# Pooled attention into soft-MoE slots: half-width w2 loads, output groups of four rows, and what goes on SyncE's queue

## The chip, the cores and the metric

The kernel runs on one core of one Trainium2 chip. The metric is the device time of one launch in microseconds (us). Every time below is in us unless it is marked ns.

## The reference

There are two stages. Attention works on 8 batches, 8 heads, 576 positions and 64 features, with keys and values averaged over blocks of 8 positions, so each head has 72 of them. Its output, 4608 rows of 512 features, is the input x of a soft mixture of experts with 8 experts, 4 slots each and 1024 hidden features.

```python
k_p = k.reshape(B, H, Sp, pool, D).mean(axis=3)          # Sp = 72, pool = 8; v_p likewise
scores = scale * np.matmul(q, k_p.transpose(0, 1, 3, 2))
attn = softmax(scores)                                   # over the 72 pooled keys
x = np.matmul(attn, v_p)                                 # -> 4608 rows of 512

logits = x @ phi                                         # 4608 x 32 slots
d = softmax(logits, axis=0)                              # over the rows
slot_input = (d.T @ x).reshape(8, 4, 512)
for e in range(8):
    h = np.maximum(slot_input[e] @ w1[e], 0.0)           # w1[e]: 512 x 1024
    slot_out[e] = h @ w2[e]                              # w2[e]: 1024 x 512
c = softmax(logits, axis=1)                              # over the 32 slots
out = c @ slot_out.reshape(32, 512)                      # 4608 x 512, fp32
```

The inputs are fp32: q, k and v of 9.4 MB each, w1 and w2 of 16.8 MB each, phi of 64 KB. The output is 9.4 MB.

## The kernel before

**Loads.** Every large input goes to SBUF by a DMA that GpSimd (POOL) issues and that casts fp32 to bf16 on the way. Their order is written out by hand and starts with k, q and v of the first pair of batches, then the next pairs, then w1 and w2. `load_pair` (L66) loads one tensor of a pair; k of pair 0 comes in two pieces (`cuts`, L98). `load_w1` (L75) loads one expert, 2 MB at the source. `load_w2` (L80) loads one expert of w2 as 8 rows of 512 columns in each partition, and with `pieces=2` it does so in two column halves, one DMA each. Experts 0 to 3 of w2 reuse the buffers of k, q and v (tag `big`), experts 4 and 5 those of the transposed queries (`qT`), experts 6 and 7 those of the attention output (`xs`). Only expert 7 comes in column halves (L385).

One load is different. SyncE (SP) issues an early piece at the very start (L93): one of the four row blocks of expert 7 of w1, 512 KB, as fp32 into `w1_f`. POOL casts it to bf16 (L102) and only then issues the loads of phi (L105) and of v of pair 0.

**Attention.** Four pairs of batches run one after another (L348). For each, TensorE (PE) pools k and v by matmuls (`pool_stage`), transposes q and computes scores; ScalarE (ACT) exponentiates; VectorE (DVE) normalizes. `place_phi` (L223) needs phi on DVE before the values can be prepared. `combine` adds the pair's part of the dispatch sum and writes its softmax weights over the slots, transposed, into `cT`.

**Experts and output.** After the last pair the order on PE, ACT, DVE and SP is that of the code. All experts' first layer (L427) is computed, then transposed into `hT`. `R_ps` (L446) holds the row sums of the combine softmax, `recR` their reciprocals. The second layer (`second`, L463) accumulates over the experts into two PSUM tiles `so_ps`, one for each half of the 512 columns, in the order in which w2 lands, with some matmuls on zeros (`warm`) between them. For expert 7 the half 0 is done first: `second`, then `slots_out` (L469) scales it into `so`, and then three output groups are written in that half; then the same for half 1.

`output` (L472) writes one group: 256 rows of the output, two consecutive ones in each partition. Two matmuls into `f_ps` (four PSUM buffers), one eviction on DVE and one on ACT into `o_sb` (six buffers), and one DMA on SP's queue. Groups 0 to 2 are written in two column halves (runs of 1 KB in HBM, 256 KB each), groups 3 to 17 in full width (runs of 4 KB, 512 KB each).

Of the kernel before, what the change touches and what calls it, by code (L numbers as in the profile page):

```python
# [8 lines left out]
FP = mybir.dt.float32  # L9
BF = mybir.dt.bfloat16  # L10
AF = mybir.ActivationFunctionType
ALU = mybir.AluOpType
# [6 lines left out]
def kernel(  # L19
# [10 lines left out]
    nc = tc.nc  # L30

    B, H, S, D = q.shape
    POOL = 8
    SP = S // POOL
    DM = H * D
    E = moe_w1.shape[0]
    F = moe_w1.shape[2]
    NS = moe_phi.shape[1]
    SPE = NS // E
    scale = 1.0 / float(D) ** 0.5  # L40
# [4 lines left out]
    NT = S // NI  # L45
    NU = NT // 2
    NR = NT // POOL
    DJ = DM // 128
    FJ = F // 128
    XW = D + NS  # L50
    HQ = H // 2
    NO = B * S // 256
    NG = 128 // NS

    consts = ctx.enter_context(tc.tile_pool(name="consts", bufs=1))
    persist = ctx.enter_context(tc.tile_pool(name="persist", bufs=1))
    big = ctx.enter_context(tc.tile_pool(name="big", bufs=4))
    qpool = ctx.enter_context(tc.tile_pool(name="qpool", bufs=2))
    xpool = ctx.enter_context(tc.tile_pool(name="xpool", bufs=2))
    ps_m = ctx.enter_context(tc.tile_pool(name="ps_m", bufs=2, space=PSUM))  # L60
# [2 lines left out]
    pool_order = ctx.enter_context(ExitStack())  # L63
    pool_order.enter_context(tc.manual_schedule(engines={ET.Pool}))

    def load_pair(src, pair, name, cuts=()):  # L66
        t = big.tile([128, NT, D], BF, name=name, tag="big")
        rows = src[2 * pair:2 * pair + 2].rearrange("b h (i t) d -> (b h i) t d", t=NT)
        for t0, t1 in zip((0,) + cuts, cuts + (NT,)):
            nc.gpsimd.dma_start(out=t[:, t0:t1], in_=rows[:, t0:t1])  # L70
        return t

    w1_sb = persist.tile([128, E, DJ, F], BF)
# [3 lines left out]

    w2_sb = [None] * E

    def load_w2(e, pool, tag, pieces=1):  # L80
        w2_sb[e] = pool.tile([128, FJ, DM], BF, name=f"w2_{tag}", tag=tag)
        src = moe_w2[e].rearrange("(p j) d -> p j d", j=FJ)
        for c in range(pieces):
            cols = slice(c * DM // pieces, (c + 1) * DM // pieces)
            nc.gpsimd.dma_start(out=w2_sb[e][:, :, cols], in_=src[:, :, cols])

    k_sb, q_sb, v_sb = [None] * NP, [None] * NP, [None] * NP


    w1_rows = moe_w1[E - 1].rearrange("(p j) f -> p j f", j=DJ)  # L90
    early = ExitStack()
    w1_f = early.enter_context(tc.tile_pool(name="early", bufs=1)).tile([128, F], FP, name="w1_f")
    nc.sync.dma_start(out=w1_f, in_=w1_rows[:, 0])  # L93


    hT = persist.tile([128, E, FJ, NS], BF)
    nc.vector.memset(hT, 0.0)
    k_sb[0] = load_pair(k, 0, "k_sb", cuts=(4 * POOL,))  # L98
    q_sb[0] = load_pair(q, 0, "q_sb")
    ident = consts.tile([128, 128], BF)  # L100
    make_identity(nc, ident)
    nc.gpsimd.tensor_copy(out=w1_sb[:, E - 1, 0], in_=w1_f)  # L102
    early.close()
    phi_f = persist.tile([128, DM // 128, NS], FP)
    nc.gpsimd.dma_start(out=phi_f, in_=moe_phi.rearrange("(p j) e -> p j e", j=DM // 128))  # L105
    v_sb[0] = load_pair(v, 0, "v_sb")


# [3 lines left out]
    def warm(n, ps):  # L112
        for _ in range(n):
            nc.tensor.matmul(out=ps, lhsT=zeros[:, 0:128], rhs=zeros, start=True, stop=True)  # L114
# [16 lines left out]
    ones = consts.tile([128, 2], BF)  # L131
# [10 lines left out]
    for r in range(2):  # L142
        rows = slice(r * D, (r + 1) * D)
        nc.vector.tensor_copy(out=iphi[rows, :, 0:D],
                              in_=ident[rows, rows].rearrange("p d -> p () d").to_broadcast([D, H, D]))


    cT = persist.tile([128, 2, B * S // 2], BF)
# [4 lines left out]
    nc.vector.memset(siT, 0.0)  # L153
    so = persist.tile([128, DM], BF)
    recC = persist.tile([128, 1], FP)
    recR = persist.tile([128, NO, 2], FP)


    for pair in range(1, NP):
        for dst, src, name in ((k_sb, k, "k_sb"), (q_sb, q, "q_sb"), (v_sb, v, "v_sb")):  # L160
            dst[pair] = load_pair(src, pair, name)
        if pair == NP - 2:
            load_w1(0)
    for e in range(1, E - 1):
        load_w1(e)
    nc.gpsimd.dma_start(out=w1_sb[:, E - 1, 1:DJ], in_=w1_rows[:, 1:DJ])
    for e in range(4):
        load_w2(e, big, "big")


    att = ExitStack()
# [7 lines left out]
    qT = [None] * NP  # L179
    xs = [None] * NP  # L180
# [105 lines left out]
    def logits(x, ee, lg, t0, t1):  # L286

        for h in range(H):
            nc.tensor.matmul(out=lg, lhsT=ident, rhs=x[:, t0:t1, h, D:XW], start=(h == 0), stop=(h == H - 1))  # L289
        nc.scalar.activation(out=ee[:, t0:t1],  # L290
                             in_=lg.rearrange("p t s -> p t () s").to_broadcast([128, t1 - t0, NG, NS]), func=AF.Exp)

# [47 lines left out]
    junk = ps_u.tile([128, 512], FP, name="junk", tag="u")  # L340
# [7 lines left out]
    for pair in range(NP):  # L348
        for qd in range(2):
            if qd == 0:  # L350
                prep = chain(prepare_kq(pair + 1), prepare_v(pair + 1)) if pair + 1 < NP else None
                if pair == 0:
                    prep = chain(prepare_v(0), prep)
            ex = [epool.tile([SP, HQ, 2, S // 2], BF, name=f"ex{b}") for b in range(2)]
            if qd == 0:
                xs[pair] = xpool.tile([128, 9, H, XW], BF, name="xs", tag="xs")
            for i in range(9):
                if i < 8:
                    score_unit(pair, i // 4 * H + qd * HQ + i % 4, ex[i // 4][:, i % 4])
                if i < 5:  # L360
                    if last is not None:
                        u_tile(*last[:2], 4 + i, last[2])
                else:
                    u_tile(pair, qd, i - 5, ex)
                step(prep)
                if pair == 0 and i % 2:
                    step(prep)
                if qd == 0 and pair > 0:
                    if i == 4:
                        comb = combine(pair - 1)  # L370
                        step(comb)
                    if i == 7:
                        step(comb)
                if qd == 1 and i in (2, 6):
                    step(comb)
            if qd == 1:
                for _ in prep or ():
                    pass
            last = (pair, qd, ex)
            if pair == NP - 2 and qd == 1:  # L380
                for e in (4, 5):
                    load_w2(e, qpool, "qT")
            if pair == NP - 1 and qd == 0:
                load_w2(E - 2, xpool, "xs")
                load_w2(E - 1, xpool, "xs", pieces=2)  # L385


    pool_order.close()
# [4 lines left out]
    junk = spare[:, 0]  # L393
# [26 lines left out]
    for n in range(E // NG):  # L420
        for half in range(F // 512):
            cols = slice(half * 512, (half + 1) * 512)
            h_ps = ps_m.tile([128, 512], FP, name="h_ps", tag="m")
            for j in range(DJ):
                for g in range(NG):
                    e = n * NG + g
                    nc.tensor.matmul(out=h_ps[g * NS:(g + 1) * NS],  # L427
                                     lhsT=siT[:, j, e * E:(e + 1) * E].rearrange("p e s -> p (e s)"),
                                     rhs=w1_sb[:, e, j, cols], start=(j == 0), stop=(j == DJ - 1),
# [13 lines left out]
    nc.vector.reciprocal(out=recC, in_=recC)  # L443


    R_ps = ps_m.tile([128, NO, 2], FP, name="R_ps", tag="m")  # L446
    for g in range(NO):
        for r in range(2):
            nc.tensor.matmul(out=R_ps[:, g, r:r + 1], lhsT=cT[:, r, g * 128:(g + 1) * 128], rhs=ones[:, 1:2],
                             start=True, stop=True)  # L450
    nc.vector.reciprocal(out=recR, in_=R_ps)
    att.close()

    opool = ctx.enter_context(tc.tile_pool(name="opool", bufs=6))
    ps_o = ctx.enter_context(tc.tile_pool(name="ps_o", bufs=1, space=PSUM))
    ps_f = ctx.enter_context(tc.tile_pool(name="ps_f", bufs=4, space=PSUM))
    CW = DM // 2
# [3 lines left out]
    def second(e, c):  # L463
        for fj in range(FJ):
            g = fj % NG
            nc.tensor.matmul(out=so_ps[c][g * NS:(g + 1) * NS], lhsT=hT[:, e, fj], rhs=w2_sb[e][:, fj, halves[c]],  # L466
                             start=(e == 0 and fj < NG), stop=(e == E - 1 and fj >= NG), skip_group_check=True)
# [4 lines left out]
    def output(g, cols):  # L472

        w = cols.stop - cols.start
        o_sb = opool.tile([128, 2, w], FP, name="o_sb", tag="o")
        f_ps = [ps_f.tile([128, w], FP, name="f_ps", tag="f") for r in range(2)]
        for r in range(2):
            nc.tensor.matmul(out=f_ps[r], lhsT=cT[:, r, g * 128:(g + 1) * 128], rhs=so[:, cols], start=True, stop=True)  # L478
        nc.vector.tensor_scalar(out=o_sb[:, 0], in0=f_ps[0], scalar1=recR[:, g, 0:1], scalar2=None, op0=ALU.mult)  # L479
        nc.scalar.activation(out=o_sb[:, 1], in_=f_ps[1], func=AF.Copy, scale=recR[:, g, 1:2])  # L480
        nc.sync.dma_start(out=out[g * 256:(g + 1) * 256].rearrange("(p r) c -> p r c", r=2)[:, :, cols], in_=o_sb)


    junk = ps_m.tile([128, 512], FP, name="junk", tag="m")
    for e in range(E - 1):
        for c in range(2):
            second(e, c)
        if e >= E - 3:
            warm(8, junk)
    for c in range(2):  # L490
        second(E - 1, c)
        slots_out(c)
        for g in range(3):
            output(g, halves[c])
    for g in range(3, NO):
        output(g, slice(0, DM))


# [28 lines left out]
```

## Time and profile before

| what | value |
|---|---|
| median of 13 runs | 180.11 us (179.34 to 181.89) |
| the profiled execution, its own time | 179.98 us |
| its span, first to last instruction | 178.0 us |
| PE, DVE, ACT, POOL busy | 138.4, 92.5, 79.8, 19.2 us |
| bytes read from HBM, written to it | 61.93 MB, 9.44 MB |
| share of DMA engine time, POOL's queue | 84.8% |
| share of DMA engine time, SP's queue | 14.6% |
| mean granted TensorE clock | 0.858 |

The page cuts the span into 40 slices of 4.45 us and gives for each the busy tenths of every engine, the mean busy tenths of the 16 DMA engines and the GB/s that they landed. A load that casts counts with its bf16 bytes. In lines of the timeline and of the chain of waits the first two numbers are the start and the duration; in brackets stands how long the engine was idle before and who released it. In the windows table each line is a stretch: its length, the busy time and count of instructions of PE, of PE's weight loads, of DVE, ACT and POOL, then PE's granted clock, the share of DMA time and GB/s. A DMA share can exceed 1 where packets overlap on an engine.

### The profile page before, as it was taken

The numbers are of one execution on the slowest core, as the hardware profiler recorded it, in microseconds if no ns is written. First come the engines' busy times: TensorE is split into PE (matmuls) and PEld (weight loads), VectorE is DVE, ScalarE is ACT, GpSimd is POOL, SyncE is SP. The second block draws the span as 40 slices with busy tenths as digits, with TensorE's granted clock in tenths as the row PEclk, the third lists the DMA queues.
The fourth block names the chain that finished last, engine by engine and source line by source line (L and its number), as shares of the span: only waits on it lengthen the run. The fifth ranks groups of instructions, "written<-read, shape, count | busy, mean of one in ns | idle before, by whom it ended". The sixth has DMA issues, their size and how long they took to land.

```text
span 178.0 us, 3540 instructions
## 1 busy us (share of the span) xinstructions
PE 138.4 (78%) x1467; PEld 85.9 (48%) x1467; DVE 92.5 (52%) x250; ACT 79.8 (45%) x144; POOL 19.2 (11%) x38
## 2 busy tenths in 40 slices
PE   4991799999999999999998987999922276774500
PEld 1361648776886587865865354644811133321100
DVE  6400650279678768869687369643700003876510
ACT  3011146988868679677697440111100002675410
POOL 6501011012110611110011111003000000000000
PEclk9999558999999999999998585589995579999555
DMA  5999999999999999999999999999999996899995
GB/s 150 171 221 225 208 223 211 220 211 221 211 222 212 222 211 219 210 219 214 215 217 214 214 214 219 214 219 215 212 215 221 209 192 81 280 396 404 407 404 229
DMA packets 10094, 40.91 MB, mean 230 GB/s; under 512 B 848, under 2 KB 4432, under 8 KB 6880
## 3 DMA queue, kind: packets, MB, share of 16 engines
q0 software_dynamic: 6144, 30.74, 84.8%
q1 hardware_dynamic: 3936, 9.96, 14.6%
q8 instruction: 11, 0.18, 0.4%
q14 instruction: 3, 0.02, 0.0%
HBM read 61.93 MB, written 9.44 MB: 401 GB/s over the span
## 4 chain that ended last, share of the span: by engine, by line
PE 44%; DMA 34%; ACT 9%; DVE 5%; issue 1%; POOL 1%; ACTq 0%; DVEq 0%
DMA w_xs<-in_moe_w_dram 17%; PE pool_ps L191 9%; PE sc L264 8%; DMA out_dram<-o_sb 7%; DMA phi_f<-in_moe_phi_dram 7%; PE u_ps L277 7%; PE G_ps L295 6%; PE q_ps L206 5%; ACT ex L265 5%; PE lg_ps L289 3%; ACT vp L256 2%; PE fold_ps L217 2%; DVE xs L283 2%; DMA w_f<-in_moe_w_dram 2%; ACT o_sb L480 1%
## 5 line engine op out<-in xcount | busy, mean ns | idle before, releaser
L265 ACT ACTIVATE ex<-sc 72x576 bf16<-72x576 f32 x64 | 38.6, 648 | 12.0 <-PE sc L264 11.1
L283 DVE TENSOR_TENSOR xs<-u_ps,rec 128x384 bf16<-128x384 f32 x72 | 39.4, 552 | 1.5
L277 PE MATMUL u_ps<-vp,ex 72*128 72x97 bf16 (+1 forms) x320 | 27.2, 221 | 1.6 <-DVE xs L283 1.5
L480 ACT ACTIVATE o_sb<-f_ps,recR 128x512 f32<-128x512 f32 (+1 forms) x21 | 12.6, 625 | 31.3 <-PE f_ps L478 27.9
L264 PE MATMUL sc<-qT,kp 64*72 64x288 bf16 x128 | 23.3, 313 | 0.8 <-ACT ex L265 0.7
L277 PEld LDWEIGHTS <-ex 72*128 72x128 bf16 (+1 forms) x320 | 18.2, 107 | 10.8 <-DVE xs L283 3.0
L282 DVE RECIPROCAL rec<-u_ps 128x4 f32<-128x4 f32 x72 | 12.5, 176 | 17.9 <-PE u_ps L277 17.4
L206 PE MATMUL q_ps<-ident,q_sb 128*128 128x128 bf16 x144 | 13.2, 242 | 4.9 <-DMA q_sb<-in_q_dram 4.2
L478 PE MATMUL f_ps<-so,cT 128*128 128x512 bf16 (+1 forms) x42 | 11.6, 371 | 6.8 <-ACT o_sb L480 4.9
L479 DVE TENSOR_SCALAR o_sb<-f_ps,recR 128x512 f32<-128x512 f32 (+1 forms) x21 | 13.6, 672 | 5.7 <-PE f_ps L478 3.1
L206 PEld LDWEIGHTS <-q_sb 128*128 128x128 bf16 x144 | 10.1, 109 | 6.6 <-DMA q_sb<-in_q_dram 4.4
L264 PEld LDWEIGHTS <-kp 64*72 64x72 bf16 x128 | 8.7, 108 | 8.3 <-issue 2.7
L295 PE MATMUL G_ps<-xs,ee 128*128 128x512 bf16 x36 | 11.8, 470 | 0.4 <-ACT ee L290 0.4
L470 DVE TENSOR_SCALAR so<-so_ps,recC 128x256 bf16<-128x256 f32 x2 | 1.0, 484 | 20.9 <-PE so_ps L466 20.9
L114 PEld LDWEIGHTS <-zeros 128*128 128x128 bf16 x53 | 5.9, 118 | 10.9 <-issue 5.8
L290 ACT ACTIVATE ee<-lg_ps 128x1152 bf16<-128x1152 f32 (+3 forms) x6 | 4.9, 811 | 13.5 <-PE lg_ps L289 13.5
L212 DVE COPY qT<-q_ps 128x768 bf16<-128x768 bf16 x16 | 8.8, 551 | 3.9 <-PE q_ps L206 3.7
L210 ACT COPY qT<-q_ps 128x768 bf16<-128x768 bf16 x8 | 6.4, 797 | 9.9 <-PE q_ps L206 9.8
L194 ACT CAST kpar<-pool_ps 128x512 bf16<-128x512 f32 (+1 forms) x12 | 5.5, 485 | 11.7 <-PE pool_ps L191 11.6
L478 PEld LDWEIGHTS <-cT 128*128 128x128 bf16 x42 | 4.0, 97 | 13.8 <-issue 11.3
L191 PE MATMUL pool_ps<-pmat,v_sb 128*128 128x128 bf16 x144 | 10.2, 227 | 0.0
L191 PE MATMUL pool_ps<-pmat,k_sb 128*128 128x128 bf16 x144 | 9.9, 219 | 0.3 <-DMA k_sb<-in_k_dram 0.2
(81 smaller groups left out, 155.2 us busy)
## 6 DMA issues: line engine op xcount, KB each, us to landing
out_dram<-o_sb SPq DMA_DIRECT2D x15, 512.0 KB, 5.0
w_sb<-in_moe_w_dram POOLq DMA_DIRECT2D x7, 1024.0 KB, 32.5
q_sb<-in_q_dram POOLq DMA_DIRECT2D x4, 1152.0 KB, 18.1
v_sb<-in_v_dram POOLq DMA_DIRECT2D x4, 1152.0 KB, 17.3
w_big<-in_moe_w_dram POOLq DMA_DIRECT2D x4, 1024.0 KB, 37.2
k_sb<-in_k_dram POOLq DMA_DIRECT2D x3, 1152.0 KB, 20.7
w_qT<-in_moe_w_dram POOLq DMA_DIRECT2D x2, 1024.0 KB, 36.2
out_dram<-o_sb SPq DMA_DIRECT2D x6, 256.0 KB, 2.6
```

The costliest lines, as they stand in the source:

```text
L191: nc.tensor.matmul(out=ps[:, r].rearrange("p n i -> p (n i)"), lhsT=src[:, tt:tt + 2, :].rearrange("p t d -> p (t d)"), rhs=pmat, start=(t ...
L206: nc.tensor.transpose(out=ps[:, t].rearrange("p n i -> p (n i)"), in_=q_sb[pair][:, tt:tt + 2, :].rearrange("p t d -> p (t d)"), identity= ...
L212: nc.vector.tensor_copy(out=dst, in_=ps)
L264: nc.tensor.matmul(out=ps[:, r, 0:S // 2], lhsT=kp[pair][rows, n], rhs=qT[pair][rows, n], start=True, stop=True)
L265: nc.scalar.activation(out=dst.rearrange("p r (i t) -> p r i t", t=NU), in_=ps[:, :, 0:S // 2].rearrange("p r (t i) -> p r i t", i=NI), fu ...
L277: nc.tensor.matmul(out=ps[rows, hh], lhsT=ex[b][:, hh].rearrange("p r t -> p (r t)")[:, c:c + rows.stop - rows.start], rhs=vp[(2 * pair + ...
L282: nc.vector.reciprocal(out=rec, in_=ps[:, :, XW])
L283: nc.vector.tensor_tensor(out=xs[pair][:, t, qd * HQ:(qd + 1) * HQ, :], in0=ps[:, :, 0:XW], in1=rec.rearrange("p h -> p h ()").to_broadcas ...
L295: nc.tensor.matmul(out=ps, lhsT=ee[:, t].rearrange("p g s -> p (g s)"), rhs=x[:, t, :, 0:D], start=(t == 0), stop=(t == 8))
L478: nc.tensor.matmul(out=f_ps[r], lhsT=cT[:, r, g * 128:(g + 1) * 128], rhs=so[:, cols], start=True, stop=True)
L479: nc.vector.tensor_scalar(out=o_sb[:, 0], in0=f_ps[0], scalar1=recR[:, g, 0:1], scalar2=None, op0=ALU.mult)
L480: nc.scalar.activation(out=o_sb[:, 1], in_=f_ps[1], func=AF.Copy, scale=recR[:, g, 1:2])
```

## The change

- The early piece of w1 is gone from SP's queue, with its buffer and POOL's cast; expert 7 of w1 is loaded whole by POOL like the others. phi is loaded by SP at the start instead. k of pair 0 is loaded in one piece, and `hT` is not cleared.
- Of the last two experts of w2, which have 8 rows each in a partition, 11 of the 16 rows are loaded in column halves: five rows of expert 6 in full width, then half 0 of its other three and of expert 7, then half 1 of both. In the second layer the two experts are taken half by half.
- Five groups of 256 rows are written in halves where three were. One group of 256 rows follows in full width. The other 3072 rows make six groups of 512 rows, four consecutive ones in each partition, so that a run in HBM is 8 KB and a DMA 1 MB; their buffers are slices of `w1_sb`.

```diff
-    w1_rows = moe_w1[E - 1].rearrange("(p j) f -> p j f", j=DJ)
-    early = ExitStack()
-    w1_f = early.enter_context(tc.tile_pool(name="early", bufs=1)).tile([128, F], FP, name="w1_f")
-    nc.sync.dma_start(out=w1_f, in_=w1_rows[:, 0])
+    phi_f = persist.tile([128, DM // 128, NS], FP)
+    nc.sync.dma_start(out=phi_f, in_=moe_phi.rearrange("(p j) e -> p j e", j=DM // 128))
...
-    nc.vector.memset(hT, 0.0)
-    k_sb[0] = load_pair(k, 0, "k_sb", cuts=(4 * POOL,))
+    k_sb[0] = load_pair(k, 0, "k_sb")
...
-    nc.gpsimd.tensor_copy(out=w1_sb[:, E - 1, 0], in_=w1_f)
-    nc.gpsimd.dma_start(out=phi_f, in_=moe_phi.rearrange("(p j) e -> p j e", j=DM // 128))
...
+    def load_last_w2(pool, tag):
+        j = FJ - 3
+        src = [moe_w2[e].rearrange("(p j) d -> p j d", j=FJ) for e in range(E)]
+        for e in (E - 2, E - 1):
+            w2_sb[e] = pool.tile([128, FJ, DM], BF, name=f"w2_{tag}", tag=tag)
+        nc.gpsimd.dma_start(out=w2_sb[E - 2][:, 0:j], in_=src[E - 2][:, 0:j])
+        for c in range(2):
+            cols = slice(c * DM // 2, (c + 1) * DM // 2)
+            nc.gpsimd.dma_start(out=w2_sb[E - 2][:, j:FJ, cols], in_=src[E - 2][:, j:FJ, cols])
+            nc.gpsimd.dma_start(out=w2_sb[E - 1][:, :, cols], in_=src[E - 1][:, :, cols])
...
-    for e in range(1, E - 1):
+    for e in range(1, E):
         load_w1(e)
-    nc.gpsimd.dma_start(out=w1_sb[:, E - 1, 1:DJ], in_=w1_rows[:, 1:DJ])
...
-                load_w2(E - 2, xpool, "xs")
-                load_w2(E - 1, xpool, "xs", pieces=2)
+                load_last_w2(xpool, "xs")
...
+    groups = []
+    for n in [2] * NSMALL + [4] * ((NO - NSMALL) // 2):       # NSMALL = 6, NHALF = 5
+        row0 = sum(128 * g[1] for g in groups)
+        step_ = n // 2
+        rows = lambda r, c0=row0 // 2, s=step_: cT[:, r % 2, c0 + r // 2:c0 + 128 * s:s]
+        groups.append((row0, n, rows))
...
+    nc.vector.memset(R_ps, 1.0)
+    for g, (_, n, rows) in enumerate(groups):
+        for r in range(n):
+            nc.tensor.matmul(out=R_ps[:, g, r:r + 1], lhsT=rows(r), rhs=ones[:, 1:2], start=True, stop=True)
...
     def output(g, cols):
         w = cols.stop - cols.start
+        row0, n, rows = groups[g]
+        if n == 4:
+            o_sb = w1_sb[:, g - NSMALL].rearrange("p j f -> p (j f)").bitcast(FP).rearrange("p (r c) -> p r c", r=n)
+        else:
+            o_sb = opool.tile([128, n, w], FP, name=f"o_sb{w}", tag=f"o{w}", bufs=2 if w == DM else 2 * NHALF)
+        for r in range(n):
+            f_ps = ps_f.tile([128, w], FP, name="f_ps", tag="f")
+            nc.tensor.matmul(out=f_ps, lhsT=rows(r), rhs=so[:, cols], start=True, stop=True)
+            if r % 2:
+                nc.scalar.activation(out=o_sb[:, r], in_=f_ps, func=AF.Copy, scale=recR[:, g, r:r + 1])
+            else:
+                nc.vector.tensor_scalar(out=o_sb[:, r], in0=f_ps, scalar1=recR[:, g, r:r + 1], scalar2=None,
+                                        op0=ALU.mult)
+        nc.sync.dma_start(out=out[row0:row0 + 128 * n].rearrange("(p r) c -> p r c", r=n)[:, :, cols], in_=o_sb)
...
-    for e in range(E - 1):
+    for e in range(E - 2):
         for c in range(2):
             second(e, c)
-        if e >= E - 3:
+        if e == E - 3:
             warm(8, junk)
     for c in range(2):
+        second(E - 2, c)
+        if c == 0:
+            warm(6, junk)
         second(E - 1, c)
         slots_out(c)
-        for g in range(3):
+        for g in range(NHALF):
             output(g, halves[c])
-    for g in range(3, NO):
+    for g in range(NHALF, len(groups)):
         output(g, slice(0, DM))
```

## The prediction

> **What bounds the kernel now.** I read the page's slices first. The DMA row stands at 9 from slice 2 to 33 and again from 36 to 39, with a dent between, and the bytes say what kind of time that is: about 215 GB/s landed while inputs come in (cast from fp32 to bf16, so twice that is read), about 405 GB/s while the output goes out. PE is as full in the middle, so I asked next who waits at the end.
>
> ```profile
> PE   4991799999999999999998987999922276774500
> DMA  5999999999999999999999999999999996899995
> GB/s 150 171 221 225 208 223 211 220 211 221 211 222 212 222 211 219 210 219 214 215 217 214 214 214 219 214 219 215 212 215 221 209 192 81 280 396 404 407 404 229
> ```
>
> In the chain of waits the last long link is a weight load, and stores follow it to the end. The PE rows of the timeline show the same: from w2's expert 3 on, each second-layer block starts when its load lands.
>
> ```profile
> 120.96 30.27 DMA w_xs<-in_moe_w_dram
> 151.28 0.43 PE so_ps L466 x8
> ...
> 136.24 1.05 PE L466 MATMUL so_ps<-w_qT,hT 128*32 128x256 bf16 x16 [4.23 <-DMA w_qT<-in_moe_w_dram]
> 141.10 1.04 PE L466 MATMUL so_ps<-w_qT,hT 128*32 128x256 bf16 x16 [3.81 <-DMA w_qT<-in_moe_w_dram]
> 148.65 0.40 PE L466 MATMUL so_ps<-w_xs,hT 128*32 128x256 bf16 x8 [0.18 <-DMA w_xs<-in_moe_w_dram]
> 151.28 0.40 PE L466 MATMUL so_ps<-w_xs,hT 128*32 128x256 bf16 x8 [0.29 <-DMA w_xs<-in_moe_w_dram]
> ```
>
> So the kernel is one stream of loads followed by one stream of stores, and what remains to be won lies at its three edges. The windows table (the last two numbers are DMA share and GB/s) prices them:
>
> ```profile
> 0.00:2.00 2.00, 0.00 (x0) 0.00 (x0) 0.98 (x2) 1.27 (x1) 0.96 (x6) 1.00 0.13 29
> 2.00:3.20 1.20, 0.94 (x3) 0.39 (x4) 1.17 (x11) 0.22 (x2) 1.20 (x3) 1.00 0.88 311
> 148.60:151.90 3.30, 1.78 (x22) 0.90 (x21) 1.99 (x5) 1.31 (x3) 0.00 (x0) 1.00 0.20 26
> 151.90:154.20 2.30, 1.60 (x9) 0.88 (x10) 1.84 (x5) 1.31 (x3) 0.00 (x0) 1.00 0.96 337
> 154.00:155.00 1.00, 0.66 (x3) 0.19 (x2) 1.00 (x2) 0.75 (x3) 0.00 (x0) 1.00 0.81 273
> 170.00:176.00 6.00, 0.00 (x0) 0.00 (x0) 0.00 (x0) 0.00 (x0) 0.00 (x0) 0.50 1.02 406
> ```
>
> **Start**: the early piece on SyncE's queue fills 1.8 to about 3.7 us. **Turn**: from 148.6 to 151.9 the DMA engines stand at 0.20. Half 0 of the last expert has landed (PE starts at 148.65) but its first store moves only at 151.9, 3.26 us later: PE, so, PE, o_sb until SP's issue at 150.66, then 1.25 us of store latency. **Stores**: 154 to 155 holds a gap of about 0.2 us between the half-0 and half-1 stores, and half-width stores (runs of 1 KB) go at 337 to 348 GB/s against 405 for full-width ones (4 KB).
>
> **What the Trainium skill says.** "DMA: Bandwidth & Descriptors", Issuing engines are not separate DMA queues: all queues end on the same 16 engines. The trace agrees: share 0.88 with SP's piece alone, 0.94 at 3.2 to 4.2 with both queues, so the piece pays only while POOL's stream is not there. The same page, Specifications: first byte about 1 us for POOL's path, 0.6 for SP's; here SP took 1.07 us (0.73 to 1.80), and POOL's own delay is hidden behind SP's packets. "Perfetto Trace Analysis", DMA Optimizations: larger pieces fill HBM bandwidth better, naming 2 KB to 4 or 8 KB; the trace agrees from 1 to 4 KB and has no 8 KB store. The first page, Where 436 GB/s comes from, puts a ceiling of 435 GB/s on what 16 engines move; no stretch here is above it once casts are counted at the source.
>
> **The change, part by part.**
>
> 1. *Early piece off SP.* 512 KB of w1 join POOL's stream. A whole w2 expert (2 MB at the source) takes 141.10 - 136.24 = 4.86 us, so a quarter costs +1.22 us. phi (64 KB) leaves that stream for SP's empty start: 4.86/32 = -0.15. POOL's cast of the piece (1.04 us) and its 0.58 us wait go, and the memset of hT (0.91 us on DVE) goes; each lies beside the loads and is worth nothing by itself.
>
> 2. *When POOL's stream starts.* Before, no slice between the two queues is empty, so the trace does not show when POOL's first descriptors were ready. Its issue is at 1.24 us. Earliest: 1.24 + the page's 1 us = 2.24; latest: as now, 3.3 to 3.7. That is a gain of 0 to 1.3 us. I take 0.5, below the middle, because the last engine decides and the share of 0.86 at 4 to 5 us says that some engines get POOL's work late even now.
>
> 3. *Column halves.* Of the last two experts' 16 rows, 8 came in halves; now 11. Eight half-rows took 151.28 - 148.65 = 2.63 us where half an expert at full width takes 2.43, so six more half-rows add 6/8 x 0.20 = +0.15. Sum of 1 to 3: loads end 1.22 - 0.15 - 0.5 + 0.15 = **+0.7 us** (-0.1 to +1.2). The distance between the landings of half 0 and half 1 grows to 11/8 x 2.63 = 3.62, so half 0 lands at +0.7 - 0.99 = **-0.3 us**, and with it the first store (3.26 us after it, the same six steps). POOL's last five DMAs, not three, are issued while over 15 us of loads are still queued (29 to 38 us from issue to landing in the tail), also where each waits for the one eight before it to land.
>
> 4. *PE order at the turn.* Expert 6's half 1 and expert 7's half 1 stand behind ten f_ps matmuls in PE's order. Those wait on four f_ps buffers, so on evictions: 10 evictions on DVE and ACT, 0.47 us each, five in a row from 1.42 us after the landing, the last matmul at about 2.9. Half 1 lands at 3.62: not late. The six warm matmuls (0.21 to 0.43 us each, 1.3 to 2.6) fit into the 2.63 us between expert 6's and expert 7's half.
>
> 5. *Half-width stores, ten in place of six.* SP issues one each 0.65 us (0.60 plus its wait), a 256 KB store at 346 GB/s lasts 0.76, so SP keeps up. The five of half 0 last until 3.26 + 3.8 = 7.06 us after the landing; half 1's first store is ready 3.62 + 3.07 = 6.69 after it (3.07 = 154.35 - 151.28: eviction to 152.59, issue at 153.1, latency 1.25). The 0.2 us gap closes, with 0.4 to spare. Four more half stores: 1.05 MB x (1/346 - 1/405) = +0.44 us.
>
> 6. *Runs of 8 KB.* Twelve full-width groups become six of 1 MB: 6.29 MB, 15.53 us at 405 GB/s. Per engine a 1 KB run costs 1024/(346/16) = 47 ns, a 4 KB run 162: 26.9 bytes per ns and 9 ns fixed. Two of 4 KB cost 324, one of 8 KB 314: -2.8%, **-0.44 us**. Ends: nothing, if rows are cut to 4 KB; -1.07 if the ceiling of 435 were reached; above zero see the last rival. Four evictions stand ahead of each store (DVE 2 x 0.75), 1.5 us against 2.6 us of transfer, and w1_sb as their buffer was read last at 125 us, so no wait on buffers. The first of them is issued about 1.3 us before the stores ahead of it run out.
>
> 7. *Rest.* R_ps's memset comes after recC in DVE's order and pushes the R matmuls and the second layer from 128.1 to about 129.3; the load that PE awaits lands at 131.40. k in one piece lets pooling begin some 1.5 us later (11.3 before; the second piece landed 10.8 us after its issue at about 1.9); q, which PE waits for next, lands at 2.46 + 15.7 = 18.2 in any case, and DVE's 12.2 us wait for phi is gone. POOL's loads are issued over 7 us ahead of their turn, so a late release starves nothing. The cT weights are now read with a step of two, by a PE that is idle half the time from 160 on. All zero.
>
> Sum: turn -0.3, gap -0.2, half stores +0.44, long runs -0.44: **-0.5 us**. Against its own time, 179.98 us (span 178.0 and 1.98 around it), that is 179.5; the median of 13 is 180.11, 0.13 above, so I predict 179.6. A measurement can tell about 0.5% here, 0.9 us: this is no change that it would see.
>
> **Rivals.**
> - *POOL starts at once* (faster). All engines get its stream at 2.2 to 2.5: loads end at +0.0, half 0 lands 1.0 earlier, stores -0.2 more: -1.2, 178.9; with 8 KB runs near the ceiling 178.2. For: POOL issues at 1.24, and SP's packets may be all that holds it. Against: the uneven 4 to 5 us.
> - *The engines drift further apart* (slower). Landings wait for the slowest of 16. At the end the share falls from 1.26 at 147.5 to 0.32 at 149.5, yet half 1 lands at 151.2: a spread of some 3 us. SP's piece gave the engines that POOL reaches late something to do. If the spread grows, both landings slip by it and the stores with them: at 1.5 us, -0.5 + 1.5 = +1.0, 181.1. It decides from 1.4 us. Against: nothing in the change touches the engines' shares of work.
> - *The long runs are no longer runs*: the queue cuts them to 4 KB, and the -0.44 is gone: 180.05, no change. If 8 KB stores fell below 371 GB/s (15.53 to 16.9 us) the result would be slower; nothing here speaks for it.
>
> **How the numbers follow.** Forecast 0.50, its own range 178.9 to 180.3; early start 0.25; drift 0.16; cut runs 0.09. Faster by over 0.5% (under 179.2): 0.25 and 0.09 of the forecast's lower edge, 0.34. Slower (over 181.0): the drift and a little of other errors, 0.18. Within: 0.48. The range 178.4 to 181.2 leaves out the ceiling case and more drift than priced.
>
> **What would show it.** Right: POOL's stream begins before 3.3 us; half 1's PE block starts at about 152.0, half 0's at 148.3; first store at 151.6; no slice under 0.9 from there; 10 half stores at 346 GB/s and the six long ones at 415. Wrong: a distance of over 4 us between the landings (then a gap opens), loads ending over 1.2 us later, or long runs at 405 or less.

## The result, and the profile after

The changed kernel took 178.05 us (median of 11 runs, 178.0 to 179.25) against 180.29 us for the kernel before (48 runs). The ratio is 0.9887, 95% interval 0.9863 to 0.9911. On a second occasion it was 178.16 against 180.48, ratio 0.9924 (0.9900 to 0.9948). The ratios leave out executions that took over 1.5% longer than the fastest of their kernel (21 of 62 of the kernel before on the second occasion), so they are not the quotients of the medians. By them the change is worth 2.0 us on the first occasion and 1.4 on the second. The forecast was 179.6, no measurable change, within 178.4 to 181.2. The kernel became about 1% faster and fell below that range. The profiled execution took 178.02 us for a span of 176.2.

The page's slices show the same shape as before, loads and then stores. The dent between them is no longer visible in the DMA row, which stays at 9, and slice 34 lands 145 GB/s where it landed 81.

```profile
DMA  4999999999999999999999999999999999999995
GB/s 76 205 224 211 226 205 220 211 216 219 215 218 211 223 211 220 210 218 218 218 208 218 221 212 212 218 218 216 212 216 219 201 196 145 317 361 425 417 417 208
```

The DMA row from 140 to 152 us, 0.3 us a digit, shows that the dent is smaller and not gone: from 148.7 to 150.2 us the engines are still busy for three to four tenths only. In the kernel before it was 0.20 for 3.3 us.

```profile
DMA  9899999999999999999999999999843333999999
```

The timeline of PE, DVE and SP at the turn (start, duration, engine, line) gives the landings.

```profile
140.05 1.05 PE L472 MATMUL so_ps<-w_qT,hT 128*32 128x256 bf16 x16 [3.80 <-DMA w_qT<-in_moe_w_dram]
...
146.79 0.40 PE L472 MATMUL so_ps<-w_xs,hT 128*32 128x256 bf16 x8 [0.18 <-DMA w_xs<-in_moe_w_dram]
147.31 0.48 DVE L476 TENSOR_SCALAR so<-so_ps,recC 128x256 bf16<-128x256 f32 x1 [20.13 <-PE so_ps L472]
...
148.82 7.65 SPq L495 DMA_DIRECT2D out_dram<-o_sb  x11
150.02 0.79 PE L472 MATMUL so_ps<-w_xs,hT 128*32 128x256 bf16 x16
150.86 0.48 DVE L476 TENSOR_SCALAR so<-so_ps,recC 128x256 bf16<-128x256 f32 x1 [0.35 <-PE so_ps L472]
```

Expert 5 of w2 lands at 140.05, where it landed at 141.10, although POOL's stream now carries 512 KB more. Half 0 follows at 146.79 in place of 148.65. SP's first store is issued 2.03 us after that, as before (2.01). `so` of half 1 comes 3.55 us after `so` of half 0, where it came 2.57 us after (149.16 and 151.73). So in these two profiles the kernel is ahead by 1.05 us before anything of the turn has begun, and by 1.86 us at half 0.

The windows table of the changed kernel (last two numbers: DMA share, GB/s) shows the start and the stores:

```profile
0.00:2.00 2.00, 0.82 (x2) 0.28 (x3) 1.11 (x11) 1.27 (x1) 0.97 (x6) 1.00 0.03 10
2.00:3.20 1.20, 1.20 (x4) 0.46 (x3) 0.33 (x3) 0.21 (x2) 1.12 (x4) 1.00 1.07 137
150.00:157.00 7.00, 5.40 (x38) 2.30 (x38) 6.17 (x12) 5.35 (x11) 0.00 (x0) 1.00 1.00 339
158.00:170.00 12.00, 3.87 (x14) 1.14 (x12) 5.03 (x8) 4.78 (x8) 0.00 (x0) 0.82 1.02 420
170.00:174.00 4.00, 0.00 (x0) 0.00 (x0) 0.00 (x0) 0.00 (x0) 0.00 (x0) 0.50 0.99 414
```

Half-width stores run without a gap at 339 GB/s (344 from 151 us on, when no load is left), and the 8 KB runs at 414 to 420 GB/s, where the 4 KB runs had 404 to 406.

The gain at the start can be read where PE first waits for q of pair 0, the second load that POOL issues. The trace records a landing of q for each of the 16 DMA engines. In the changed kernel the last of them is at 15.97 us and PE starts on q at 16.02: it waits for the slowest engine. The kernel before:

```profile
18.24 1.46 PE L206 MATMUL q_ps<-ident,q_sb 128*128 128x128 bf16 x12 [4.23 <-DMA q_sb<-in_q_dram]
```

The changed kernel:

```profile
16.02 4.27 PE L206 MATMUL q_ps<-ident,q_sb 128*128 128x128 bf16 x33 [3.29 <-DMA q_sb<-in_q_dram]
```

That is 2.22 us. Less the piece's 1.22 us, which POOL loads later, and with the 0.15 us of phi that it no longer loads, 1.15 is left, and 1.05 is what expert 5 shows.

The 16 landings tell where it comes from. "Middle" is the median of the 16 engines, "last" the slowest.

| profile | q, middle | q, last | expert 5, middle | expert 5, last |
|---|---|---|---|---|
| before | 15.85 | 18.20 | 138.74 | 141.06 |
| before, second profile | 15.48 | 18.14 | 138.17 | 140.99 |
| changed | 14.73 | 15.97 | 138.62 | 140.01 |
| changed, second profile | 14.75 | 15.72 | 138.57 | 140.06 |

At q the middle engine is 1.12 us earlier: POOL's first packets start at 2.62 us in place of 3.30, and the piece's are not among them. By expert 5 that is used up, since the piece has to be loaded after all: the middle engine stands at 138.62 against 138.74. What stays is the lag of the last engine behind the middle one, 2.35 us at q before and 1.24 after. From q to expert 5 the first and the last engine drift apart by a further 0.9 to 2.3 us in every profile, so one landing of expert 5 is not exact: with the start of the changed kernel it lies between 139.85 and 140.73 in eight profiles. q is the surer sign.

### The profile page after: what moved, and what is told of

Same layout as the page of the kernel before. It is cut to its first block, busy times and chain, and to the rows that moved or that the text cites. A ratio compares the mean times of both kernels' runs of the same rounds, so it can differ in the third digit from the quotient of the medians.

```text
span 176.2 us, 3525 instructions
## 1 busy us (share of the span) xinstructions
PE 137.8 (78%) x1469; PEld 86.0 (49%) x1469; DVE 90.6 (51%) x252; ACT 79.9 (45%) x146; POOL 18.5 (10%) x37
## 4 chain that ended last, share of the span: by engine, by line
PE 49%; DMA 25%; ACT 13%; DVE 4%; issue 2%; POOL 0%; ACTq 0%; DVEq 0%; POOLq 0%
DMA w_xs<-in_moe_w_dram 17%; PE pool_ps L191 9%; PE sc L264 8%; DMA q_sb<-in_q_dram 8%; PE u_ps L277 7%; PE G_ps L295 6%; PE q_ps L206 6%; ACT ex L265 5%; PE f_ps L489 3%; PE lg_ps L289 3%; ACT w_sb L491 2%; ACT vp L256 2%; DVE xs L283 2%; PE fold_ps L217 2%; ACT o_sb L491 2%
## 5 line engine op out<-in xcount | busy, mean ns | idle before, releaser
L491 ACT ACTIVATE o_sb<-f_ps,recR 128x256 f32<-128x256 f32 (+1 forms) x11 | 5.2, 492 | 26.8 <-PE f_ps L489 26.8
L489 PE MATMUL f_ps<-so,cT 128*128 128x512 bf16 (+1 forms) x46 | 11.0, 331 | 3.5 <-DVE so L476 1.2
L472 PEld LDWEIGHTS <-hT 128*32 128x32 bf16 x128 | 3.5, 104 | 13.0 <-issue 12.8
L191 PEld LDWEIGHTS <-v_sb 128*128 128x128 bf16 x144 | 9.0, 104 | 0.8 <-issue 0.2
```

The source lines that it names most:

```text
L191: nc.tensor.matmul(out=ps[:, r].rearrange("p n i -> p (n i)"), lhsT=src[:, tt:tt + 2, :].rearrange("p t d -> p (t d)"), rhs=pmat, start=(t ...
L489: nc.tensor.matmul(out=f_ps, lhsT=rows(r), rhs=so[:, cols], start=True, stop=True)
L491: nc.scalar.activation(out=o_sb[:, r], in_=f_ps, func=AF.Copy, scale=recR[:, g, r:r + 1])
```

## The experiments

The question was where the 2 us came from: from the start, the turn or the long runs, and which of the start's four edits it was. Each kernel below is the changed kernel with one thing put back, unless said otherwise.

**Old start.** All four edits of the start undone.

```diff
-    nc.sync.dma_start(out=phi_f, in_=moe_phi.rearrange("(p j) e -> p j e", j=DM // 128))
+    nc.sync.dma_start(out=w1_f, in_=w1_rows[:, 0])
+    nc.vector.memset(hT, 0.0)
-    k_sb[0] = load_pair(k, 0, "k_sb")
+    k_sb[0] = load_pair(k, 0, "k_sb", cuts=(4 * POOL,))
+    nc.gpsimd.tensor_copy(out=w1_sb[:, E - 1, 0], in_=w1_f)
+    nc.gpsimd.dma_start(out=phi_f, in_=moe_phi.rearrange("(p j) e -> p j e", j=DM // 128))
...
```

> The changed kernel with the old start alone: early piece of w1 on SP's queue, phi on POOL's, k of pair 0 in two pieces, hT cleared. Theory A (the gain is mainly at the start: POOL's stream begins earlier and its slowest engine catches up, by more than the early piece was worth): w2's expert 5 lands at about 141.1 us again instead of 140.05, all later steps follow by about 1.05, ratio to the kernel before about 0.9945 (179.3 us). Theory B (the start is worth nothing, the turn and the long runs brought all of it): ratio stays at 0.988 to 0.989.

Measured: 179.24 us, ratio 0.9959 (0.9934 to 0.9985). Its PE rows:

```profile
17.85 1.46 PE L216 MATMUL q_ps<-ident,q_sb 128*128 128x128 bf16 x12 [4.20 <-DMA q_sb<-in_q_dram]
...
141.83 1.04 PE L482 MATMUL so_ps<-w_qT,hT 128*32 128x256 bf16 x16 [3.87 <-DMA w_qT<-in_moe_w_dram]
```

q is late again and so is expert 5. Theory A holds: the start is worth some 1.1 us by the medians (179.24 against 178.05 to 178.16) and 0.6 to 1.3 us by the ratios, about half of the gain or more. But single runs went from 177.83 to 180.72, so some executions with the old start were as fast as the changed kernel.

**Old turn.** Expert 7 alone in halves, three half-width groups, warm matmuls as before.

```diff
-    NHALF = 5
+    NHALF = 3
-        j = FJ - 3
+        j = FJ
...
```

> The changed kernel with the old turn alone: expert 7 of w2 in column halves only, three groups in half width, six rows of warm matmuls back where they were. From the prediction's own terms the first store comes 0.99 us later after the loads, the 0.2 us gap is back and four half stores fewer give 0.44 back: +0.75 us against the changed kernel, ratio to before about 0.993 (178.8 us). A rival, that the turn is hidden by something else and worth nothing: 0.989.

Measured: 179.67 us, ratio 0.9985 (0.9961 to 1.0009), far more than expected. The timeline and the window of that run show that the edit had made a new wait:

```profile
158.41 0.69 ACT L490 ACTIVATE o_sb<-f_ps,recR 128x512 f32<-128x512 f32 x1 [2.43 <-DMA out_dram<-o_sb]
158.43 0.75 DVE L492 TENSOR_SCALAR o_sb<-f_ps,recR 128x512 f32<-128x512 f32 x1 [2.73 <-DMA out_dram<-o_sb]
```

```profile
158.00:160.00 2.00, 0.86 (x3) 0.29 (x3) 1.57 (x3) 1.27 (x2) 0.00 (x0) 0.61 0.53 215
```

With three half-width groups, three groups of 256 rows follow in full width, and `opool` has only two buffers for them. Both evicting engines stand still until a store gives one back, and DMA falls to 0.53. So it was run again with a third buffer.

```diff
-bufs=2 if w == DM else 2 * NHALF
+bufs=3 if w == DM else 2 * NHALF
```

> As the run with the old turn (expert 7 of w2 alone in column halves, three groups in half width), but with three buffers for the three full-width groups of 256 rows in place of two. In that run DVE and ACT stood still for 2.7 and 2.4 us at 158.4, until a store gave its buffer back, and DMA at 0.53 from 158 to 160; about 0.9 us of store time were lost so. Without it: +0.75 us against the changed kernel, by the prediction's terms, ratio to before 0.991 to 0.994. If the ratio stays at 0.9985, the turn is worth twice what the prediction said.

Measured: 178.29 us, ratio 0.9912 (0.9887 to 0.9937). The turn by itself is worth 0.1 to 0.25 us by the medians, where the prediction's terms made 0.75. Against the two ratios of the changed kernel it is +0.45 and -0.2 us, so it is not clear of zero.

**Runs of 4 KB.** Twelve groups of 256 rows in the same buffers.

```diff
-    NSMALL = 6
+    NSMALL = NO
...
```

> The changed kernel with twelve full-width groups of 256 rows (runs of 4 KB, 512 KB a store) in the same buffers in place of the six of 512 rows. If the fixed cost per run is the cause: stores at 405 GB/s in place of 415 to 419, +0.44 to +0.6 us, ratio to before 0.991 to 0.992. If the long runs bring nothing: 0.989.

Measured: 178.2 us, ratio 0.9916 (0.9885 to 0.9947), which does not stand clear of the changed kernel; the span is 176.4. Its windows:

```profile
158.00:170.00 12.00, 3.85 (x14) 1.10 (x12) 5.01 (x8) 4.76 (x8) 0.00 (x0) 0.85 1.02 405
170.00:174.00 4.00, 0.00 (x0) 0.00 (x0) 0.00 (x0) 0.00 (x0) 0.00 (x0) 0.50 1.02 406
```

The rate is the one expected, 405 in place of 414 to 420. But the time is not all there. The DMA rows from 172 to 176 us, 0.1 us a digit, with each packet counted where it starts, show where each kernel's packets run out. The changed kernel:

```profile
DMA  1991997999799799799000000000000000000000
```

With runs of 4 KB:

```profile
DMA  9996999959979999699698995800000000000000
```

By their records the last packets end at 174.2 and at 174.8 us, but the spans at 176.2 and 176.4. Of 0.6 us of store time only 0.2 reach the end. After the last packet the changed kernel goes on for 2.0 us, the other for 1.6. The reason for that difference was not tried, and the length of the stores is not it alone: with the same stores of 1 MB at the end, both runs of the old turn went on for only 1.3 us.

**More halves.** 14 of the last 16 rows in halves, six half-width groups.

```diff
-        j = FJ - 3
+        j = FJ - 6
-    NHALF = 5
+    NHALF = 6
```

> The changed kernel with 14 of the last 16 rows of w2 in column halves and six half-width groups. The landings of the two halves stand 14/8 x 2.63 = 4.6 us apart, half 0 lands 0.85 us earlier and the first store with it, while loads still run on the slower engines. If the stretch with idle engines at the turn is filled so: up to -0.6 us against the changed kernel (ratio to before 0.985 to 0.987). If the stores only take the bandwidth that the last loads need, or more 1 KB runs eat it up: 0.989 or above.

Measured: 177.85 us, ratio 0.9896 (0.9854 to 0.9939), no difference from the changed kernel.

```profile
144.90 1.87 PE L116 MATMUL junk<-zeros 128*128 128x512 bf16 x6
146.71 0.40 PE L472 MATMUL so_ps<-w_xs,hT 128*32 128x256 bf16 x8
...
151.04 0.40 PE L472 MATMUL so_ps<-w_xs,hT 128*32 128x256 bf16 x8 [0.27 <-DMA w_xs<-in_moe_w_dram]
```

Half 0's block starts at 146.71, hardly before the changed kernel's 146.79, and half 1's waits for DMA until 151.04. The blocks did move apart, by 4.33 us (4.6 expected), but mostly because half 1 moved back. Half 0's last landing is recorded at 146.4, 0.3 us before its block, which starts when the warm matmuls end. Eight half-rows took 2.63 us in the kernel before where full rows take 2.43, and the last loads now run beside the first stores, which begin at 150.0. No more was to be won here from halving more than 11 rows.

**The start, edit by edit.** Four kernels put back one of its edits each, and two put back the piece with one partner each.

```diff
 piece_back:    nc.sync.dma_start(out=w1_f, in_=w1_rows[:, 0]) ahead of phi; POOL's cast
 cuts_back:     k_sb[0] = load_pair(k, 0, "k_sb", cuts=(4 * POOL,))
 memset_back:   nc.vector.memset(hT, 0.0)
 phi_on_pool:   nc.gpsimd.dma_start(out=phi_f, ...) behind q, nothing on SP's queue
 piece_cuts, piece_memset: two of these together
```

> The changed kernel with the early piece of w1 alone put back: SP loads it first, phi behind it on SP's queue; k in one piece, no memset of hT. Theory A1 (SP's packets stand ahead of POOL's on each engine and hold POOL's stream until 3.3 us and later, most on the engines that POOL reaches last): first POOL packets at 3.2 to 3.4 in place of 2.6, k's landing spread over the engines by about 3 us in place of 1.6, w2's expert 5 at 141.1 to 141.8 us in place of 140.05, ratio to before 0.994 to 0.996. Theory A2 (the memset of hT or the two pieces of k delayed POOL's stream, and the piece itself only filled empty time): expert 5 at 139.0 to 139.3, ratio 0.983 to 0.985.

> The changed kernel with k of pair 0 in two pieces again, nothing else. A1: the stream starts at 2.6 as in the changed kernel, expert 5 lands within 0.5 us of 140.05, ratio 0.987 to 0.990. A2 with the pieces as the cause: slowest engine 1 to 2 us later, ratio 0.994.

> The changed kernel with the memset of hT on DVE again (0.91 us from about 1 us on, while POOL writes its first descriptors), nothing else. A1: no effect, expert 5 within 0.5 us of 140.05, ratio 0.987 to 0.990. A2 with the memset as the cause: POOL's first packets at 3.2 us or later, expert 5 up to 1 us later, ratio 0.993.

> The changed kernel with nothing on SP's queue at the start and phi on POOL's queue behind q. A1, with any SP packets at the start as the cause: POOL's stream starts earlier still than 2.6 us; otherwise it starts at 2.6 and phi adds 0.15 us: expert 5 at 140.2, ratio 0.988 to 0.991.

> The changed kernel with the early piece on SP's queue and k of pair 0 in two pieces, without the memset. Alone neither delayed the loads (expert 5 at 139.78 and 140.33 us against 140.05), all of the old start together did (141.83). Theory C1 (it takes both: three POOL loads stand behind SP's packets on each engine when they start, and some engines are served late): k whole on the slowest engine at about 12 us in place of 10.2, expert 5 at 141 us or later, ratio to before 0.992 to 0.996. Theory C2 (it takes the memset or phi on POOL's queue): expert 5 at 139.8 to 140.4, ratio 0.983 to 0.988.

> The changed kernel with the early piece on SP's queue and the memset of hT, k in one piece. C1: like the piece alone, expert 5 at 139.8 to 140.3, ratio 0.983 to 0.988. C2 with the memset as the partner: expert 5 at 141 or later, ratio 0.992 to 0.996.

The landings of q and of expert 5 are the starts of PE's blocks, as in the lines above. In the first two rows phi is on POOL's queue too.

| kernel | piece on SP | k in two | memset | q of pair 0 | expert 5 | median us | ratio (95%) |
|---|---|---|---|---|---|---|---|
| before | yes | yes | yes | 18.24 | 141.10 | 180.29 | |
| old start | yes | yes | yes | 17.85 | 141.83 | 179.24 | 0.9959 (0.9934 to 0.9985) |
| piece and two pieces of k | yes | yes | no | 18.25 | 142.08 | 178.31 | 0.9921 (0.9896 to 0.9946) |
| piece and memset | yes | no | yes | 18.14 | 141.98 | 177.81 | 0.9872 (0.9828 to 0.9916) |
| piece | yes | no | no | 16.34 | 139.78 | 177.89 | 0.9832 (0.9790 to 0.9873) |
| k in two pieces | no | yes | no | 15.40 | 140.33 | 177.92 | 0.9850 (0.9816 to 0.9883) |
| memset | no | no | yes | 15.89 | 140.98 | 179.02 | 0.9893 (0.9849 to 0.9937) |
| phi on POOL | no | no | no | 15.93 | 140.11 | 178.23 | 0.9875 (0.9838 to 0.9911) |
| changed | no | no | no | 16.02 | 140.05 | 178.05 | 0.9887 (0.9863 to 0.9911) |

The profiled executions of the two kernels with one partner took 180.11 and 180.16 us, about 2 us above their medians, so their landings are shown but decide nothing. Without any of the piece, q lands by 16.13 in every profile, those of the other experiments included. With the piece alone it lands 0.3 us later than in the changed kernel, and since POOL's later loads are 1.22 us shorter, expert 5 is even early. Half of theory A1 holds for the piece alone: POOL's first packets start later, at 3.57 us in place of 2.62 (3.2 to 3.4 foretold). But the engines finished k 1.25 us apart and not 3, and expert 5 was not late. A2 falls too, for neither the memset nor the two pieces of k delays q. With all the edits of the old start together q is 1.8 to 2.2 us late in each of three profiles (18.24 and 17.85 here, 18.18 below). Which combination it takes, C1 or C2, stays open: by its ratio neither pair stands clear of the changed kernel, and no run has the piece with phi on POOL's queue alone.

**Repeats.** Since single runs of the kernels with the piece scattered, three kernels were run once more.

> The changed kernel again, as the yardstick for the three others. Ratio to before 0.987 to 0.990, all its runs within about 1.3 us of each other (178.0 to 179.25 before); k whole on the slowest engine at about 10.2 us, spread over the engines at most 1.6 us, as in all nine profiles without the early piece.

> The changed kernel with the early piece alone put back, again. The kernels with the piece ran from 176.8 to 180.7 us, those without it within 0.5 to 1.3 us of their median, and of five profiles with the piece four had some engines 2.3 to 2.8 us behind the first when k had landed, this one 1.3. Theory D1 (the piece makes the start uneven in some executions and not in others, so that its 1.22 us are won or lost by chance): times again spread over 2 us or more on both sides of the changed kernel's, median within 0.3% of it. Theory D2 (the piece alone is harmless and worth its bytes, only its combination with the two pieces of k or the memset costs): every run under the changed kernel's, ratio 0.980 to 0.984, spread under 1.4 us.

> The kernel before, a second profile of it. D1: its slowest engine again 2 us or more behind at the landing of k, or not at all, and w2's expert 5 within 139.5 and 142 us accordingly. If the start is the same in every execution: expert 5 at 141.10 again, within 0.2 us. Ratio to itself 0.998 to 1.002.

The changed kernel came out at 178.16, its runs from 177.8 to 178.91, q at 15.77. The kernel before came out at 179.9, its runs from 178.64 to 181.59, ratio to itself 1.0017 (0.9988 to 1.0045); q at 18.18 and expert 5 at 141.03. That is within 0.1 us of its first profile. So both profiles of the kernel before start late; whether all its executions do is not shown, since its times go from 178.1 to 182.75 us. The piece alone:

```profile
16.04 0.84 PE L213 MATMUL q_ps<-ident,q_sb 128*128 128x128 bf16 x12 [3.31 <-DMA q_sb<-in_q_dram]
...
139.51 1.05 PE L479 MATMUL so_ps<-w_qT,hT 128*32 128x256 bf16 x16 [3.94 <-DMA w_qT<-in_moe_w_dram]
```

177.86 us, runs from 177.3 to 179.61, ratio 0.9904 (0.9871 to 0.9937). In both profiles of the piece alone expert 5 is 0.3 to 0.5 us early. Its middle engine is 0.6 to 0.7 us early (137.88 and 137.98 against 138.62), so the piece does pay there. But the kernel's times scatter over 2.3 us where the changed kernel's scatter over 1.1. D1 is nearer than D2: the median is 0.2% under the changed kernel's and single runs lie on both sides of it.

**Half a piece, and piece with more halves.**

```diff
 half_piece:   nc.sync.dma_start(out=w1_f, in_=w1_rows[:, 0:F // 2])
 piece_halves: piece_back with  j = FJ - 6  and  NHALF = 6
```

> The changed kernel with an early piece of half the size (256 KB of w1, phi behind it on SP's queue), k in one piece. In the changed kernel POOL's first packets start at 2.6 us and SP's queue can move data from about 1.75, so this piece fills just the empty stretch. If the piece pays as far as it ends before POOL's stream starts: POOL's first packets at 2.7 to 3.0, k's spread under 1.6 us, expert 5 at about 139.6, 0.4 to 0.6 us under the changed kernel, times within 1.5 us of each other, ratio to before 0.985 to 0.988. If any SP packet at the start delays POOL's stream by as much as it carries: as the changed kernel, 0.988 to 0.992.

> The changed kernel with the whole early piece back (k in one piece, no memset) and with 14 of the last 16 rows of w2 in halves and six half-width groups: the two edits that stood at or under the changed kernel's time. If both add: 0.3 us for the piece, 0.2 for the halves, ratio to before 0.984 to 0.988, single runs from 176.8 to 179.5 as with the piece. If the start's scatter and the stores' lower rate eat them up: 0.988 to 0.992.

Measured: half the piece 178.24 us, ratio 0.9877 (0.9835 to 0.9919), q at 16.36, expert 5 at 139.81. Piece and more halves 177.87 us, ratio 0.9868 (0.9825 to 0.9911), q at 17.05, expert 5 at 140.86. Neither stands clear of the changed kernel, and the two edits do not add. In the second kernel the piece came back alone, and q was still 1 us late, with the engines 2.0 us apart. So the piece by itself can make the start uneven, if less than the whole old start. No version was found that surely beats the changed kernel.

**The new start in the kernel before.** The other direction: the kernel before with the new start alone.

```diff
-    nc.sync.dma_start(out=w1_f, in_=w1_rows[:, 0])
+    nc.sync.dma_start(out=phi_f, in_=moe_phi.rearrange("(p j) e -> p j e", j=DM // 128))
-    nc.vector.memset(hT, 0.0)
-    k_sb[0] = load_pair(k, 0, "k_sb", cuts=(4 * POOL,))
+    k_sb[0] = load_pair(k, 0, "k_sb")
...
```

> The kernel before with the new start alone (no early piece, phi on SP, k in one piece, no memset), its turn and its stores of 4 KB unchanged. If the start brings 1.05 to 1.8 us by itself, as the landings of expert 5 say (140.05 against 141.10 in the kernel before and 141.83 with the old start): ratio 0.990 to 0.994, expert 5 at about 140. If the start pays only together with the new turn: 0.998 to 1.002.

Measured: 179.17 us, ratio 0.9975 (0.9953 to 0.9997). Expert 5 landed at 140.03, as foreseen, but the ratio gives 0.45 us, less than half of that microsecond. The profiled execution (181.01 us, 1.8 us above the median) showed a suspect:

```profile
145.55 1.04 PE L458 MATMUL so_ps<-w_xs,hT 128*32 128x256 bf16 x16 [0.95 <-DMA w_xs<-in_moe_w_dram]
146.52 3.37 PE L107 MATMUL junk<-zeros 128*128 128x512 bf16 x8
149.82 0.40 PE L458 MATMUL so_ps<-w_xs,hT 128*32 128x256 bf16 x8
```

The eight warm matmuls of the kernel before at this place:

```profile
146.57 1.90 PE L114 MATMUL junk<-zeros 128*128 128x512 bf16 x8
```

They took 1.90 us there and 3.37 here, where the clock is 0.50 from 148 to 149 us, and half 0's block begins the moment they end. So they were taken away.

```diff
-        if e >= E - 3:
+        if e == E - 3:
             warm(8, junk)
```

> The kernel before with the new start, and without the eight warm matmuls between expert 6's block and half 0 of expert 7. With them the profile showed half 0's block at 149.82 us, behind 3.37 us of warm matmuls at half clock, though its load had landed at about 147.2 by the landing of the pieces. Theory E1 (these matmuls held PE up and hid the gain of the start in that kernel): half 0's block waits for DMA again, at about 147.3, ratio to before about 0.990, against 0.9975 with them. Theory E2 (the start brings little in this kernel): ratio stays at 0.997.

Measured: 179.54 us, ratio 0.9987 (0.9966 to 1.0008): not faster. Half 0's block did wait for DMA, as E1 said, and came at 147.91 (147.3 expected; expert 5 was at 140.43 this time). But look at a window of its stores, where the sixth number after the length is PE's clock:

```profile
153.00:154.00 1.00, 0.96 (x4) 0.30 (x3) 0.60 (x3) 0.78 (x2) 0.00 (x0) 0.50 0.46 169
```

PE runs at half clock, 96% busy, while DMA stands at 0.46 in the middle of the stores. E1 falls as the whole reason: what the earlier half 0 won was lost behind it.

The half clock is not peculiar to this kernel. The second profile of the changed kernel (178.14 us) and the profile of the old turn with a third buffer (178.95 us) have it at the turn as well:

```profile
150.00:157.00 7.00, 6.32 (x34) 2.56 (x33) 5.01 (x11) 4.28 (x9) 0.00 (x0) 0.51 0.97 332
```

```profile
151.00:158.00 7.00, 6.38 (x25) 2.22 (x18) 5.23 (x9) 4.14 (x8) 0.00 (x0) 0.51 0.88 313
```

The changed kernel keeps DMA at 0.97 there, against 1.00 at full clock, and the old turn falls to 0.88. This suggests that the old turn, with three half-width groups, loses part of the start's gain in a half-clock stretch and that the new turn loses little. Since no kernel here sets the clock, it is not shown.

## Why the prediction was wrong

- **Step 1**, the bytes: right. With the piece alone put back, the middle engine is 0.56 us later at q and 0.74 us earlier at expert 5 than in the changed kernel. That makes 1.3 us for the piece, where 1.22 was forecast.
- **Step 2**, when POOL's stream starts, is the step that failed. It took a gain of 0.5 us and at most 1.3, and step 7 let q land at 18.2 "in any case". q came 2.2 us earlier, at 16.02. Half of that, 1.12 us on the middle engine, is the earlier stream: it lies inside the range of step 2, which had taken 0.5. The other half, 1.11 us, is the shorter lag of the slowest engine. Step 2 named the last engine as a reason to take less, but the sum put its lag at no change, and only the rival of the drifting engines had it, with the other sign. Steps 1 and 2 gave +0.57 us at expert 5 and steps 1 to 3 -0.3 at half 0; measured was -1.05 and -1.86. This one term is 1.6 us off, and the distance between 179.6 and 178.05 is 1.55.
- **The start's edits were priced one by one**, in steps 1 and 7, with k in one piece and the memset at zero. No one of them alone moves the time clear of the changed kernel. The old start as a whole does (its interval, 0.9934 to 0.9985, against 0.9863 to 0.9911; it touches that of the second occasion), so the cost lies in a combination, which the sum did not contain. Why the slowest engine lags with it stays open.
- **POOL's first packets** came 1.4 us after the issue (1.23 to 2.62). The earliest time of step 2, 2.24, had allowed 1 us for this; the measured figure decides. Pooling of k, which step 7 put 1.5 us later, began at 10.55 us in place of 11.50.
- **Steps 3 and 4**, the distance of the halves: 3.62 forecast, 3.55 measured. The 2 us from the landing to SP's first issue stayed as forecast.
- **Step 5**: the gap closed, and half-width stores went at 339 to 344 GB/s (346 assumed).
- **Step 6**: 8 KB runs at 414 to 420, forecast 415. The rate was right, but undoing it moved the span by only 0.2 us, not 0.44.
- **The turn's net worth** was forecast at about -0.75 us and found at -0.1 to -0.25 by the medians when undone alone, not clear of zero. The start's -1.1, the turn's and the runs' come to -1.2 to -1.5, against -1.4 to -2.0 for the whole by the ratios. A rest that belongs to their working together is possible but not shown. The new start in the kernel before, with 0.45 us and then none, points to it.
- **The rivals**: "POOL starts at once" foretold the sign and, at 178.9 to 178.2, nearly the size, and the middle engine's 1.12 us are what it speaks of. That 178.2 comes so close is luck: it supposed stores near 435 GB/s, and they stayed at 414 to 420, while the lag of the slowest engine, which it did not count, gave the rest. SP's piece alone does hold POOL's first packets (3.57 us against 2.62), but it held q back by only 0 to 1.0 us of the 2.2, so it is not all that held the stream. The feared drift of the engines went the other way: the lag was larger in the kernel before, and the change removed about half of it.

## What to carry to other kernels

In a kernel bound by one DMA stream, judge a change of the first microseconds by the landing of the second or third load, which is when the slowest engine is done, not by when the first bytes move. Ahead of such a stream, keep few transfers. Here pieces that each cost nothing clear on their own came with slow engines when they were together, and the stream, never idle again, carried the lag to its last load (the engines finished q 2.65 us apart in the kernel before and expert 5 3.56 us apart). When undoing one part of a change, look for the wait that the undoing itself makes (here a third buffer).

## What was not expected of the hardware

- With an early 512 KB transfer on SP's queue, k in two pieces, a memset on DVE and phi on POOL's queue, the second load landed 1.8 to 2.2 us later than without, in three profiles (18.24, 18.18, 17.85 against 16.02 and 15.77), and 120 us on, expert 5 was still late, although 512 KB fewer lay before it in POOL's stream.
- Stores in runs of 1, 4 and 8 KB moved at 339, 405 and 414 to 420 GB/s.
- Kernels with the early piece scatter over 2.3 us and more from run to run (piece alone 176.8 to 179.59 and 177.3 to 179.61). Those without it mostly scatter over 0.5 to 1.9 us, but two with the old turn over some 3 us.
- From the end of the last packet to the end of the span passed 2.0 us in the changed kernel, 1.7 in the kernel before, and 1.3 in the kernels with the old turn put back.
